# Third normalised block's square root earlier with read-outs on VectorE, the check's sums in the second pair, and second products of five groups by Strassen's seven products

## The chip, the cores and the metric

The kernel runs on 1 core of one Trainium2 chip. The metric is the device time of one execution in microseconds (us). Before the change it is 712.18 us, the median of three runs (710.34 to 712.77).

## What is computed

`x` has 2048 rows (S) of 512 columns (D); the hidden width F of the gated part is 1792. Cut to what matters:

```python
mod = (silu(c) @ w_mod).reshape(1, 6, 1, -1)
sa, ca, ga, sb, cb, gb = (mod[:, i] for i in range(6))
h = layernorm(x) * (1 + ca) + sa
a, b = h @ dft_hid_re.T, h @ dft_hid_im.T
x = x + ga * (dft_seq_re @ a - dft_seq_im @ b)
h = layernorm(x) * (1 + cb) + sb
x = x + gb * ((silu(h @ w1) * (h @ w3)) @ w2)
```

All of it is float32. The kernel multiplies in a rounded 32-bit format and writes each factor as a high part and a low rest, so that a product is three matmuls: high by high, high by low, low by high.

## The kernel before

The first 262 us of the profile are the Fourier part: it uses the symmetry of the transform matrices, and a check (`square`, `judge`) sums squares on the side, from which a flag `bad` is made; at the very end the program branches on it to a general version that needs no symmetry. The rest, about 436 us, is the gated part. That is where the change lies.

There the 2048 rows stand as four blocks t = 0 to 3 of 512 columns each (rows of `x` are the matmuls' moving columns). Two blocks make a pair: pair 0 is blocks 0 and 2, pair 1 is blocks 1 and 3. F is cut into seven groups g of 256, and a group has two factors (w1 and w3, 128 columns each twice) and one second product (w2).

- Groups 0 and 1 of pair 0 are done plainly (`up_block`), block 0 first, then block 2: `up(0, 0)`, `up(1, 0)`, eight second products of block 0, `up(0, 2)`, `up(1, 2)`. Here "the third block" is block 2; its normalisation (`ln2(2)`) must be done when `up(0, 2)` starts.
- Everything else is twelve items: groups 2 to 6 of pair 0, then groups 0 to 6 of pair 1. In an item each factor is done by Strassen's scheme in Winograd's form (`factor`), seven products in place of eight, called a1 to a7 for w1 and b1 to b7 for w3. One such unit is six matmuls. The second products are plain before the change (`down_unit`): for each of two blocks t and four slices d one unit of six matmuls in a bank of its own, and one read-out that scales by `gb` (`copy_by`, on ScalarE, line 335) into a tile `y`. Two read-outs fill a `y`, which GpSimd's queue adds to a sum in DRAM by an accumulating DMA (line 1146). Groups 5 and 6 of pair 1 add into the loaded sums `xr` instead and store the output.

The order on TensorE is written out by hand: the string `body` for an item lists its units, with a `y` where a second product of the item before is put between. `-b7`, `-b4`, `-b3` are units of the item before. ScalarE and VectorE get their own work in the order in which the planner's loop emits it. Two lists feed it beside the units: `jobs` (splitting weights into high and low) and `background` (the normalisations `ln2`, line 880 and around it). A step has a cost in us, and `advance` emits steps until the credit of a unit is used up; `pause` ends a turn. `behind(n, fn)` emits fn n units later. Each engine then executes its instructions strictly in that order.

The steps of `ln2` that matter: `a6` is a square root on ScalarE (32 by 16 numbers, with a table load ahead of it), `a6b` the reciprocal and its spread over the partitions on VectorE, `a7(i)` two multiplications on VectorE, `a8(i)` scale and shift on ScalarE, and then `chunk_parts` makes the high parts `h2h` (ScalarE) and the rests `h2l` (VectorE), which are what `up_block` multiplies.

Tiles of 512 KB come from a list of 50 slots (`take`, `give`), first in, first out; a slot that a `y` held is handed out again four units after its unit, and its next writer waits for the DMA that read it.

Of the kernel before, what the change touches and what calls it, by code (L numbers as in the profile page):

```python
# [8 lines left out]
F32 = mybir.dt.float32  # L9
# [33 lines left out]
def folded(nc, pools, c, cp, wmr, wmc, x, xt, ctr, cti, wdr, wdi, w1, w3, w2, out):  # L43
# [773 lines left out]
    def ln2(t):  # L817
# [97 lines left out]
        apart = t != PAIRS[0][0]  # L915
        pause = (0, None, 0.0, 0.0)
        for slots, fn, dve, act in (
# [17 lines left out]
            pause,  # L935
# [13 lines left out]
    def chunk_parts(queue, t, i, more=0):  # L949
# [8 lines left out]

        step(queue, 1 + more, highs, 0.0, 1.0)
# [153 lines left out]
    down_banks = [4, 4]  # L1113

    def down_unit(g, pair, t, d, key):
# [7 lines left out]
        for n in range(parts):  # L1123
            at = slice(n * N // parts, (n + 1) * N // parts)
            to = bank(down_banks[0] + turn[1] % down_banks[1])[:, at]
# [16 lines left out]
            else:  # L1142
                copy_by(ys[0][:, d % 2, :], to, gb[:, d : d + 1])
# [66 lines left out]

    def right(pair, n):
# [7 lines left out]
    def result(i, w, q, k, src):  # L1219
# [6 lines left out]
        times(v, v, src)  # L1226

# [9 lines left out]
        behind(2, lows)  # L1237

    def factor(i, w, n):
# [37 lines left out]
        if n == 3:  # L1277
            for x in wuse.pop(key).values():
                give(x)
            behind(1, lambda: give(st["x"]))  # L1280
            if w == "w3":
                for x in vs.pop(i):
                    behind(3, lambda x=x: give(x))
# [239 lines left out]
    for n, (j, k) in enumerate(steps):  # L1523
# [4 lines left out]
        for m in range(2):  # L1528
# [9 lines left out]
            if (j, k, m) == (0, NK - 1, 1):  # L1538
                for t in PAIRS[0]:
                    ln2(t)  # L1540
                    for i in range(2):
                        chunk_parts(background, t, i, 1)
# [36 lines left out]
    def down(g, pair, t, d, key):  # L1579
        drain(lambda: (key, "l") in done, jobs)  # L1580
        delayed()
        down_unit(g, pair, t, d, key)
# [14 lines left out]
    judge()  # L1597
# [8 lines left out]
    down_banks[:] = [6, 2]  # L1606
# [13 lines left out]

    def unit(kind, i, n):
# [12 lines left out]
        if (kind, n) == ("a", 1) and more:  # L1634
            load_w(("w1", *items[i + 1]))
        if (kind, n) == ("a", 6):
            load_w(("w2", g, pair))
        if (kind, n) == ("a", 3) and more:
            load_w(("w3", *items[i + 1]))
            weight_jobs(i + 1, "w1")  # L1640
        if (kind, n) == ("b", 2):
            plain_jobs(("w2", g, pair))
        if (kind, n) == ("b", 3):
# [7 lines left out]
            if more:  # L1651
                weight_jobs(i + 1, "w3")
            for t in PAIRS[pair]:
                seconds.extend((g, pair, t, d, ("w2", g, pair)) for d in range(ND))
# [5 lines left out]
    for i in range(len(items)):  # L1660
        body = "a6 a5 y a7 y y a4 y a3 y b1 y b2 y b6 b5 y"
        if i == turning:
            body = "y y y y y a6 y a5 y a7 y b1 b2 a4 b6 a3 b5"
        if i == len(items) - 1:
            body = "a6 a5 y a7 y y a4 y a3 b1 y b2 b6 b5 y b7 y b4 y b3 y y y y y y y y"
        head = "-b7 a1 -b4 -b3 a2 " if i == turning else "-b7 a1 a2 -b4 -b3 " if i else "a1 a2 "
# [813 lines left out]
```

## Time and profile before

| | |
|---|---|
| median of three runs | 712.18 us (710.34 to 712.77) |
| the profiled execution | 708.46 us |
| its span, first to last instruction | 706.7 us |
| mean granted TensorE clock | 0.991 |
| HBM read, written | 76.81 MB, 33.55 MB |
| accumulating DMAs `sum<-y` | 48 of 512 KB, median 5.6 us to landing |

The profile is of one execution. Busy times are a share of the span; PE is TensorE's matmuls, PEld its weight loads, DVE VectorE, ACT ScalarE, POOL GpSimd. A matmul's own duration overlaps that of the next one, so the pitch from start to start is what counts. In brackets behind a row of a timeline stands the idle time of its engine just before it and what ended it. DMA share is the mean busy share of the 16 DMA engines.

### The profile page before, as it was taken

The numbers are of one execution on the slowest core, as the hardware profiler recorded it, in microseconds if no ns is written. First come the engines' busy times: TensorE is split into PE (matmuls) and PEld (weight loads), VectorE is DVE, ScalarE is ACT, GpSimd is POOL, SyncE is SP. The second block draws the span as 40 slices with busy tenths as digits, with TensorE's granted clock in tenths as the row PEclk, the third lists the DMA queues.
The fourth block names the chain that finished last, engine by engine and source line by source line (L and its number), as shares of the span: only waits on it lengthen the run. The fifth ranks groups of instructions, "written<-read, shape, count | busy, mean of one in ns | idle before, by whom it ended". The sixth has DMA issues, their size and how long they took to land.

```text
span 706.7 us, 8912 instructions
## 1 busy us (share of the span) xinstructions
PE 686.3 (97%) x3152; PEld 564.7 (80%) x3152; DVE 548.3 (78%) x877; ACT 430.8 (61%) x709; POOL 119.4 (17%) x141
## 2 busy tenths in 40 slices
PE   7999999999999999899999999999999999999995
PEld 4898888888888888687888788787788888888784
DVE  5999679997999978579987886896865556664763
ACT  4998865545454655745677676867665565656420
POOL 1320253542524000200100101011010100101000
PEclk9999999999999999999999999999999999999998
DMA  8730299796678521522868558376763847537403
GB/s 266 211 120 1 77 373 328 251 307 229 207 283 287 168 86 41 92 58 64 209 114 199 89 130 153 61 156 137 239 136 73 180 62 175 111 69 162 137 0 124
DMA packets 38100, 108.93 MB, mean 154 GB/s; under 512 B 4896, under 2 KB 5152, under 8 KB 38048
## 3 DMA queue, kind: packets, MB, share of 16 engines
q0 software_dynamic: 12352, 43.00, 29.3%
q1 hardware_dynamic: 25264, 63.98, 27.5%
q10 hardware_dynamic: 432, 1.31, 0.5%
q8 instruction: 26, 0.43, 0.3%
q14 instruction: 26, 0.21, 0.1%
HBM read 76.81 MB, written 33.55 MB: 156 GB/s over the span
## 4 chain that ended last, share of the span: by engine, by line
PE 81%; DVE 7%; ACT 6%; issue 2%; DMA 2%; SPq 1%; ACTq 0%; DVEq 0%
PE bank L100 52%; PE bank L750 25%; PE bank L559 2%; PE bank L598 1%; DMA wmr<-in_wmr 1%; ACT xc L894 1%; PE bank L576 1%; DVE xc L96 1%; SPq L231 1%; ACT hf L87 1%; ACT y L335 1%; DVE v L96 0%; DVE hl L90 0%; ACT hm L501 0%; DMA w<-in_wdi 0%
## 5 line engine op out<-in xcount | busy, mean ns | idle before, releaser
L100 PE MATMUL bank<-hf,w2h 128*128 128x512 f32 (+1 forms) x452 | 140.9, 391 | 0.3
L1146 POOL DMA_DIRECT2D sum<-y x48 | 41.0, 855 | 390.1 <-ACT y L335 373.0
L100 PEld LDWEIGHTS bank<-hf,w2h 128*128 128x128 f32 x452 | 84.3, 188 | 22.1 <-DVE hf L90 3.4
L100 PE MATMUL bank<-hf,w2l 128*128 128x512 f32 (+1 forms) x226 | 87.6, 388 | 0.0
L87 ACT ACTIVATE hf<-v 128x512 fp32r<-128x512 f32 x56 | 35.3, 630 | 67.3 <-DVE v L96 62.7
L335 ACT ACTIVATE y<-bank,gb 128x512 f32<-128x512 f32 x96 | 64.9, 682 | 18.6 <-PE bank L100 18.3
L93 DVE TENSOR_TENSOR v<-bank,x 128x512 f32<-128x512 f32 x36 | 24.7, 685 | 34.9 <-PE bank L100 34.8
L750 PE MATMUL bank<-bh,us 128*128 128x512 f32 x128 | 49.9, 390 | 0.0
L93 DVE TENSOR_TENSOR x<-bank,x 128x512 f32<-128x512 f32 x36 | 24.7, 687 | 32.4 <-PE bank L100 28.7
L750 PE MATMUL bank<-bh,ul 128*128 128x512 f32 x128 | 49.8, 389 | 0.0
L750 PE MATMUL bank<-d,us 128*128 128x512 f32 x128 | 49.8, 389 | 0.0
L750 PE MATMUL bank<-d,uh 128*128 128x512 f32 x128 | 49.8, 389 | 0.0
L750 PE MATMUL bank<-l,us 128*128 128x512 f32 x128 | 49.8, 389 | 0.0
L750 PE MATMUL bank<-l,uh 128*128 128x512 f32 x128 | 49.8, 389 | 0.0
L100 PEld LDWEIGHTS bank<-hf,w2l 128*128 128x128 f32 x226 | 42.4, 188 | 8.4
L90 DVE TENSOR_TENSOR hf<-v,hf 128x512 fp32r<-128x512 f32 x56 | 38.5, 687 | 12.2 <-ACT hf L87 12.1
L170 POOL DMA_INDIRECT re<-in_ctr,mirror x32 | 35.8, 1117 | 66.2 <-DVE ul L90 39.5
L1224 ACT ACTIVATE v<-v 128x512 f32<-128x512 f32 x36 | 22.8, 632 | 38.8 <-DVE v L93 38.8
L87 ACT ACTIVATE x<-bank 128x512 f32<-128x512 f32 x72 | 41.4, 586 | 7.2 <-PE bank L100 6.5
L170 POOL DMA_INDIRECT im<-in_cti,mirror x32 | 32.7, 1023 | 35.3 <-PE bank L750 10.0
L100 PE MATMUL bank<-h2h,w1h 128*128 128x512 f32 x80 | 31.8, 397 | 1.5 <-ACT h2h L87 1.5
L100 PE MATMUL bank<-h2l,w1h 128*128 128x512 f32 x80 | 31.9, 399 | 0.8 <-DVE h2l L90 0.8
(246 smaller groups left out, 1775.2 us busy)
## 6 DMA issues: line engine op xcount, KB each, us to landing
sum<-y POOLq DMA_DIRECT2D x48, 512.0 KB, 5.6
w<-in_w SPq DMA_DIRECT2D x42, 512.0 KB, 4.5
re<-in_ctr SPq DMA_DIRECT2D x32, 256.0 KB, 5.0
im<-in_cti SPq DMA_DIRECT2D x32, 256.0 KB, 5.0
wmc<-in_wmc SPq DMA_DIRECT2D x8, 512.0 KB, 6.3
xr<-in_xt SPq DMA_DIRECT2D x8, 512.0 KB, 7.6
sum<-xr SPq DMA_DIRECT2D x8, 512.0 KB, 6.2
x<-in_x SPq DMA_DIRECT2D x11, 256.0 KB, 4.8
```

Source lines behind the costliest of these rows:

```text
L87: nc.scalar.activation(dst, src, AF.Copy, scale=scale)
L90: nc.vector.tensor_tensor(out=dst, in0=a, in1=b, op=OP.subtract)
L93: nc.vector.tensor_tensor(out=dst, in0=a, in1=b, op=OP.add)
L96: nc.vector.tensor_tensor(out=dst, in0=a, in1=b, op=OP.mult)
L100: nc.tensor.matmul(acc, lhs[a], rhs[b], start=first and n == 0, stop=last and n == len(PASSES) - 1, skip_group_check=more,)
L170: nc.gpsimd.indirect_dma_start(dst, None, rows, bass.IndirectOffsetOnAxis(ap=at, axis=0))
L231: queue.dma_start(raw_w[dt][q * 64 : (q + 1) * 64, m, :], w[i][par::2, q])
L335: nc.scalar.activation(dst, src, AF.Identity, scale=by)
L559: nc.tensor.matmul(halves(hb[k])[:, m, :], sides((hh, hl)[a][k])[:, dt, m, :], wu[dt][:, b, m, :], start=False, stop=dt % 2 == 1 and n == ...
L750: nc.tensor.matmul(acc[what, e], lhs, rhs, start=begin and i == 0, stop=(end or (turn and what == "x")) and i == len(terms) - 1, skip_grou ...
L1146: nc.gpsimd.dma_start(sums[t, d // 2], y, accum_op=OP.add)
L1224: behind(k != 0 or q == 0, lambda: nc.scalar.activation(v, src, AF.Silu))
```

## The change

Four parts:

1. **Third block.** For block 2 (`rushed`) the pauses around `a6` to `a8` and their costs go, and the two chunks' `h2h` and `h2l` are emitted with them. Read-outs `y` number 1 to 4 of each block's second products in pair 0's first groups go from ScalarE to VectorE (the new line 1153).
2. **The check.** `judge()` is called in the second item of pair 1, behind b4, in place of just ahead of `up(0, 2)`.
3. **Second products.** For groups 0 to 4 of pair 1 (`SEVEN`), w2's four quarters and the four quarters of `silu(gate) * up` are combined by Strassen's scheme as the factors are: seven units of two times three matmuls in banks 6 and 7 in place of eight units of six. Sums of a bank go on over several units, so each unit is read out from both banks (14 read-outs in place of 8), and each gives a `y` and a DMA (7 in place of 4). w2 gets `totals` and split sums, as w1 and w3 have.
4. **Order.** New strings for pair 1: in most of it two factor units between two second products, w1's loads and jobs placed anew, w3's jobs three units sooner, the last item's second products over five banks.

```diff
+        rushed = t == PAIRS[0][1]
...
-            pause,
+            *[pause] * (not rushed),
             (0, a6, 0.0, 2.8),
             pause,
             (0, a6b, 1.6, 0.0),
-            (0, lambda: a7(0), 1.2, 0.0),
-            *[pause] * apart,
-            (0, lambda: a8(0), 0.0, 1.4),
-            (0, lambda: a7(1), 1.2, 0.0),
-            *[pause] * apart,
-            (0, lambda: a8(1), 0.0, 1.4),
+            *[pause] * rushed,
+            (0, lambda: a7(0), 1.2 * (not rushed), 0.0),
+            *[pause] * (apart and not rushed),
+            (0, lambda: a8(0), 0.0, 1.4 * (not rushed)),
+            (0, lambda: a7(1), 1.2 * (not rushed), 0.0),
+            *([(0, fn, 0.0, 0.0) for fn in (None, chunk(t, 0)[0], None)] if rushed else [pause] * apart),
+            (0, lambda: a8(1), 0.0, 1.4 * (not rushed)),
...
+        if rushed:
+            for fn in (chunk(t, 0)[1], None, chunk(t, 1)[0], None, chunk(t, 1)[1], None):
+                step(background, 0, fn)
...
-                copy_by(ys[0][:, d % 2, :], to, gb[:, d : d + 1])
+                if pair == 0 and 1 <= g * ND + d <= 4:
+                    nc.vector.tensor_scalar(
+                        ys[0][:, d % 2, :], to, gb[:, d : d + 1], None, op0=OP.mult
+                    )
+                else:
+                    copy_by(ys[0][:, d % 2, :], to, gb[:, d : d + 1])
...
+    SEVEN = [(g, 1) for g in range(NG - 2)]
+    ORDER7 = (2, 5, 3, 1, 6, 7, 4)
+    LEFT7 = {1: "h0", 2: "h2", 4: "h3", 5: "s0", 6: "s1", 7: "s2", 3: "s3"}
+    TO7 = {2: (0, 0), 5: (1, 1), 3: (0, 1), 1: (0, 0), 6: (0, 1), 7: (1, 1), 4: (1, 0)}
...
+    def seven_parts(i, q, k):
...
+        t1, t2, t3, t4 = v[0, 0], v[1, 1], v[0, 1], v[1, 0]
+        behind(1, lambda: minus(t1, v[0, 1], v[0, 0]))
+        behind(2, lambda: high(5, t1))
+        behind(2, lambda: minus(t3, v[1, 1], v[0, 1]))
+        behind(3, lambda: low(5, t1))
+        behind(3, lambda: minus(t2, v[1, 1], t1))
+        behind(4, lambda: high(7, t3))
+        behind(4, lambda: minus(t4, v[1, 0], t2))
...
+    def seven_jobs(key):
...
+    def seven_unit(g, pair, n, key):
+        new = n in (1, 2, 5)
+        if new:
+            banks7[:] = [bank(6), bank(7)]
+        y = take(F32, "y")
...
+        for e, to in enumerate(banks7):
+            at = int(LEFT7[n][1]) * HALF + e * P
+            product(
+                to,
+                [flat(wuse[key][x])[:, at : at + P] for x in names],
+                [u[:, b, :] for b in range(2)],
+                new,
+                True,
+                not new,
+            )
+            d = 2 * which + e
+            copy_by(y[:, e, :], to, gb[:, d : d + 1])
+        give(u)
+        nc.gpsimd.dma_start(sums[t, which], y, accum_op=OP.add)
+        behind(4, lambda: give(y))
...
-    judge()
     up(0, 2)
...
+        if (kind, i, n) == ("b", turning + 1, 4):
+            judge()
...
+        if not more and kind == "a" and state[i, "w1"]["n"] == 7:
+            down_banks[:] = [6, 7, 0, 1, 2]
...
+        if i and items[i - 1] in SEVEN:
+            body = "a6 a5 a7 y a3 a4 y b1 b2 y b6 b5 y"
+        spread = i > 1 and items[i - 2] in SEVEN
+        if spread and i < len(items) - 1:
+            body = body.replace("a6", "a6 y", 1)
+        if i == len(items) - 2:
+            body = "a6 y a5 y a7 a3 y a4 b1 y b2 b6 y b5"
...
-            body = "a6 a5 y a7 y y a4 y a3 b1 y b2 b6 b5 y b7 y b4 y b3 y y y y y y y y"
+            body = "a6 a5 a7 a3 a4 b1 b2 y b6 y b5 y b7 y b4 y y b3 y y y y y y y y y y"
...
+        if spread and i < len(items) - 1:
+            head = "-b7 a1 y a2 -b4 y -b3 "
```

What this does to the order, at three places. The first is ScalarE ahead of `up(0, 2)`: `s` holds block 2's variances, `y` the second products of block 0 that are read out, `xc` block 2's two halves, and the last row is the table load ahead of the SiLU of `up(0, 2)`. Before:

```order
L87 ACTIVATE hf_379_2737<-v_377_2714 128x512
L880 ACT_TABLE_LOAD
L880 ACTIVATE s_2_377_2721<-s_2_377_2721,eps_128 32x16
L335 ACTIVATE y_381_2743<-bank4_382_2744,gb_152 128x512
L335 ACTIVATE y_381_2743<-bank5_383_2759,gb_152 128x512
L335 ACTIVATE y_384_2769<-bank6_385_2770,gb_152 128x512
L894 ACTIVATE xc_348_2564<-xc_348_2564,sb_150,cb1_151 128x512 x2
L335 ACTIVATE y_384_2769<-bank7_386_2780,gb_152 128x512
L335 ACTIVATE y_387_2790<-bank4_388_2791,gb_152 128x512
L894 ACTIVATE xc_360_2611<-xc_360_2611,sb_150,cb1_151 128x512 x2
L335 ACTIVATE y_387_2790<-bank5_389_2801,gb_152 128x512
L335 ACTIVATE y_390_2810<-bank6_391_2811,gb_152 128x512
```

and now:

```order
L880 ACT_TABLE_LOAD
L880 ACTIVATE s_2_377_2721<-s_2_377_2721,eps_128 32x16
L87 ACTIVATE hf_379_2738<-v_377_2714 128x512
L335 ACTIVATE y_381_2750<-bank4_382_2751,gb_152 128x512
L894 ACTIVATE xc_348_2564<-xc_348_2564,sb_150,cb1_151 128x512 x2
L87 ACTIVATE h2h_384_2772<-xc_348_2564 128x1024
L894 ACTIVATE xc_360_2611<-xc_360_2611,sb_150,cb1_151 128x512 x2
L87 ACTIVATE h2h_389_2796<-xc_360_2611 128x1024
L335 ACTIVATE y_390_2798<-bank5_393_2809,gb_152 128x512
L335 ACTIVATE y_394_2819<-bank6_395_2820,gb_152 128x512
L335 ACTIVATE y_394_2819<-bank7_396_2829,gb_152 128x512
L1103 ACT_TABLE_LOAD
```

The table load and the root stand ahead of `hf`. Before, seven read-outs stand ahead of the first `h2h` (it is the next row); now one does.

The second is VectorE at the same place. Before, from block 0's last product of the two factors on:

```order
L96 TENSOR_TENSOR v_377_2714<-v_377_2714,bank3_378_2723 128x512
L90 TENSOR_TENSOR hf_379_2737<-v_377_2714,hf_379_2737 128x512
L883 RECIPROCAL s_2_377_2721<-s_2_377_2721 32x16
L847 COPY w_2_382_2753<-s_2_377_2721 32x16 x4
L848 STREAM_TRANSPOSE stat_347_2556<-w_2_382_2753 128x512
L96 TENSOR_TENSOR xc_348_2564<-xc_348_2564,stat_347_2556 128x1024
L96 TENSOR_TENSOR xc_360_2611<-xc_360_2611,stat_347_2556 128x1024
L90 TENSOR_TENSOR h2l_393_2821<-xc_348_2564,h2h_392_2819 128x1024
L90 TENSOR_TENSOR h2l_396_2834<-xc_360_2611,h2h_395_2832 128x1024
L1006 TENSOR_REDUCE sq_2836<-chk_82 128x8
```

and now:

```order
L96 TENSOR_TENSOR v_377_2714<-v_377_2714,bank3_378_2724 128x512
L883 RECIPROCAL s_2_377_2721<-s_2_377_2721 32x16
L847 COPY w_2_379_2741<-s_2_377_2721 32x16 x4
L848 STREAM_TRANSPOSE stat_347_2556<-w_2_379_2741 128x512
L90 TENSOR_TENSOR hf_379_2738<-v_377_2714,hf_379_2738 128x512
L96 TENSOR_TENSOR xc_348_2564<-xc_348_2564,stat_347_2556 128x1024
L96 TENSOR_TENSOR xc_360_2611<-xc_360_2611,stat_347_2556 128x1024
L1153 TENSOR_SCALAR y_381_2750<-bank5_383_2763,gb_152 128x512
L1153 TENSOR_SCALAR y_385_2774<-bank6_386_2775,gb_152 128x512
L90 TENSOR_TENSOR h2l_387_2785<-xc_348_2564,h2h_384_2772 128x1024
L1153 TENSOR_SCALAR y_385_2774<-bank7_388_2787,gb_152 128x512
L1153 TENSOR_SCALAR y_390_2798<-bank4_391_2799,gb_152 128x512
```

The reciprocal passes `hf`, four read-outs come in, and the check's sums (L1006 and on) are gone from behind `h2l`.

The third is ScalarE in the second pair, from the first splitting of a group's w2 on. Before:

```order
L87 ACTIVATE w2h_829_5232<-w2_805_5104 128x1024
L87 ACTIVATE hf_831_5236<-v_797_5055 128x512
L335 ACTIVATE y_832_5238<-bank6_833_5239,gb_152 128x512
L87 ACTIVATE x_825_5210<-bank3_824_5203 128x512
L87 ACTIVATE x_835_5262<-bank5_834_5255 128x512
L335 ACTIVATE y_832_5238<-bank7_836_5264,gb_152 128x512
L87 ACTIVATE hf_837_5281<-v_798_5056 128x512
L87 ACTIVATE x_839_5290<-bank0_838_5283 128x512
```

and now:

```order
L87 ACTIVATE w2h_796_5014<-w2_773_4898 128x1024
L87 ACTIVATE hf_798_5021<-v_765_4815 128x512
L335 ACTIVATE y_799_5023<-bank6_789_4982,gb_152 128x512
L335 ACTIVATE y_799_5023<-bank7_790_4983,gb_152 128x512
L87 ACTIVATE w2sh_801_5035<-w2s_797_5016 128x1024
L87 ACTIVATE x_794_5003<-bank3_793_4996 128x512
L87 ACTIVATE w3h_803_5047<-w3_784_4959 128x1024
L87 ACTIVATE x_805_5056<-bank5_804_5049 128x512
L335 ACTIVATE y_809_5065<-bank6_807_5063,gb_152 128x512
L335 ACTIVATE y_809_5065<-bank7_808_5064,gb_152 128x512
L87 ACTIVATE w3sh_811_5077<-w3s_806_5058 128x1024
L87 ACTIVATE hf_812_5087<-v_766_4816 128x512
```

Read-outs come in pairs and there are more of them, `w2sh` is new, and `w3h` and `w3sh` stand ahead of the first pieces of `hf` of that group.

More of the change, by code (lines that the diff above doesn't have):

```diff
@@ L1650, in unit @@
                 other_operands()
-            if more:
+            if more and not early_w3(i):
                 weight_jobs(i + 1, "w3")
-            for t in PAIRS[pair]:
-                seconds.extend((g, pair, t, d, ("w2", g, pair)) for d in range(ND))
+            if (g, pair) in SEVEN:
+                seconds.extend((g, pair, n, ("w2", g, pair)) for n in ORDER7)
+            else:
+                for t in PAIRS[pair]:
+                    seconds.extend((g, pair, t, d, ("w2", g, pair)) for d in range(ND))
+        if (kind, n) == ("b", 6) and more and early_w3(i):
+            weight_jobs(i + 1, "w3")
         beside(1.36, FACTOR[kind][n])
```

100 lines of the change are left out of this document (87 added, 13 removed).

## The prediction

> **What bounds the kernel now.** I read the page first, then the windows, then TensorE's waits and its timeline. The page's busy times and the chain's shares:
>
> ```profile
> span 706.7 us, 8912 instructions
> PE 686.3 (97%) x3152; PEld 564.7 (80%) x3152; DVE 548.3 (78%) x877; ACT 430.8 (61%) x709; POOL 119.4 (17%) x141
> PE 81%; DVE 7%; ACT 6%; issue 2%; DMA 2%; SPq 1%; ACTq 0%; DVEq 0%
> PE bank L100 52%; PE bank L750 25%; PE bank L559 2%; PE bank L598 1%; DMA wmr<-in_wmr 1%; ACT xc L894 1%; PE bank L576 1%; DVE xc L96 1%; SPq L231 1%; ACT hf L87 1%; ACT y L335 1%; DVE v L96 0%; DVE hl L90 0%; ACT hm L501 0%; DMA w<-in_wdi 0%
> ```
>
> TensorE sets the time: 81% of the chain is matmuls, 52% of the span those of line 100, the gated part. A matmul taken out of there is worth its pitch, as long as nothing new holds the engine up. The pitch is read from the timeline of the first block, where `up(0, 0)` runs without a gap:
>
> ```profile
> 262.38 0.39 PE L100 MATMUL bank<-h2h,w1h 128*128 128x512 f32 x1
> 270.54 0.39 PE L100 MATMUL bank<-h2h,w3h 128*128 128x512 f32 x1
> ...
> 698.47 0.28 PE L100 MATMUL bank<-hf,w2l 128*128 128x256 f32 x1
> ```
>
> From the first matmul of w1's first quarter to the first of w3's second quarter are three blocks of twelve, 36 matmuls in 8.16 us: 0.2267 us each; a unit of six is 1.36 us. The gated part needs 192 matmuls of the plain `up`, 12 items of 84, and 14 times 48 second products, 1872 in all: 424.4 us. It lasts from 262.38 to the end of the last row, 698.75 us: 436.4 us, so 12 us in it are lost. The largest piece stands ahead of `up(0, 2)` (PE's timeline):
>
> ```profile
> 294.80 0.39 PE L100 MATMUL bank<-hf,w2l 128*128 128x512 f32 x1
> 296.71 0.51 PE L100 MATMUL bank<-h2h,w1h 128*128 128x512 f32 x1 [1.53 <-ACT h2h L87]
> 297.97 0.79 PE L100 MATMUL bank<-h2l,w1h 128*128 128x512 f32 x1 [0.76 <-DVE h2l L90]
> 298.56 0.63 PE L100 MATMUL bank<-h2h,w1l 128*128 128x512 f32 x1
> 300.70 0.50 PE L100 MATMUL bank<-h2l,w1h 128*128 128x512 f32 x1
> 295.00:300.00 5.00, 2.72 (x7) 0.75 1.02 193
> 300.00:305.00 5.00, 5.00 (x22) 0.91 0.71 107
> ```
>
> (The last two rows are of the windows of PE alone: busy, count, granted clock.) TensorE waits for block 2's `h2h`, then for `h2l`; then the granted clock is down and five matmuls from 298.56 to 300.70 go at 0.43 us each.
>
> **Third block: -4.2 us.** From 294.80 to 300.70 nine matmuls started where 26 would have fitted; eight steps at 0.2267 us are 1.8 us of the 5.9 us, so 4.1 us are lost, and 0.1 us more in the step behind. To see whether the new order ends it I walk the queues with these rows (ACT, then DVE):
>
> ```profile
> 281.62 0.60 ACT L1094 ACTIVATE v<-bank 128x512 f32<-128x512 f32 x1 [0.24 <-PE bank L100]
> 285.13 0.63 ACT L87 ACTIVATE hf<-v 128x512 fp32r<-128x512 f32 x1 [2.91 <-DVE v L96]
> 285.78 1.28 ACT L880 ACT_TABLE_LOAD   x1
> 287.29 1.82 ACT L335 ACTIVATE y<-bank,gb 128x512 f32<-128x512 f32 x3
> 290.49 1.53 ACT L894 ACTIVATE xc<-xc,sb,cb 128x512 f32<-128x512 f32 x2 [1.37 <-issue]
> 295.61 1.05 ACT L87 ACTIVATE h2h<-xc 128x1024 fp32r<-128x1024 f32 x1
> 284.02 0.25 DVE L840 TENSOR_REDUCE s<-q 32x16 f32<-32x64 f32 x1
> 284.41 0.69 DVE L96 TENSOR_TENSOR v<-v,bank 128x512 f32<-128x512 f32 x1
> 288.43 0.71 DVE L848 STREAM_TRANSPOSE stat<-w 128x512 f32<-128x512 f32 x1
> 289.18 2.36 DVE L96 TENSOR_TENSOR xc<-xc,stat 128x1024 f32<-128x1024 f32 x2
> 296.69 1.23 DVE L90 TENSOR_TENSOR h2l<-xc,h2h 128x1024 fp32r<-128x1024 f32 x1 [5.15 <-ACT h2h L87]
> ```
>
> Now the table load may start at 282.2, where ACT only waits for `v`, and is over when the variances `s` come at 284.3; the root ends at 284.7. DVE does the reciprocal behind `v` at 285.1, the spread until 286.8, `hf` until 287.5, both `xc` until 289.8 (291.5 before). ACT has `hf` and one read-out behind it by 286.5, shifts the first `xc` from 288.7, has the first `h2h` at 291.1 and the second at 293.6. DVE: read-outs of 0.7 us at 289.8 and 290.5, the first `h2l` at 292.4, two read-outs, the second `h2l` at 295.0. `up(0, 2)` can start at 295.0 and needs the second half 1.4 us later: no wait, and no lowered clock. Four read-outs come on DVE; no row of before has that form, and I price it between ACT's `y` (0.61 us each of 1.82 us for three) and DVE's `v<-v,bank` (0.69 us), at 0.7. They lie in the 5.15 us in which DVE waits for `h2h`. The read-outs left to ACT end at 296.1, the table load at 297.4, and the SiLU behind it is due at 297.9. A table load that turned out 1.5 us longer would still only touch that SiLU.
>
> [...]
>
> **The check: 0.** Its first and last VectorE instruction are, in DVE's timeline,
>
> ```profile
> 299.70 0.42 DVE L1006 TENSOR_REDUCE sq<-chk 128x8 f32<-128x256 f32 x1 [0.27 <-POOL sq L1005]
> 302.66 0.14 DVE L1026 TENSOR_SCALAR bad<-fine 1x1 int32<-1x1 f32 x1
> ```
>
> 3.1 us for small instructions that follow each other's results; TensorE has no wait there but the one it already had. In the second pair they stand behind b4's product; the next thing TensorE needs from DVE there is b3's sum, two units (2.7 us) on, which feeds products that come seven units later. Without that cover it is 3.1 us once.
>
> **Second products: -6.8 us.** Seven units in place of eight, in five groups: 5 x 6 = 30 matmuls at 0.2267 us. What they add per group goes to engines that are not full. Five stretches of 30 us, each about one group, and their groups:
>
> ```profile
> 540.00:570.00 30.00, 30.00 (x133) 24.57 (x132) 17.68 (x28) 18.17 (x27) 3.40 (x4) 1.00 0.60 123
> sum 150.00, PE 150.00 PEld 122.81 DVE 88.45 ACT 90.61 POOL 17.03; mean PE 30.00 PEld 24.56 DVE 17.69 ACT 18.12 POOL 3.41
> L335 ACT ACTIVATE y<-bank,gb 128x512 f32<-128x512 f32 x40 | 27.4, 684 | 10.4 <-PE bank L100 10.3
> L87 ACT ACTIVATE hf<-v 128x512 fp32r<-128x512 f32 x20 | 12.7, 633 | 23.2 <-DVE v L96 21.9 <-issue 1.3
> L87 ACT ACTIVATE w1sh<-w1s 128x1024 fp32r<-128x1024 f32 x5 | 5.3, 1063 | 0.6
> L90 DVE TENSOR_TENSOR hf<-v,hf 128x512 fp32r<-128x512 f32 x20 | 13.7, 686 | 3.5 <-ACT hf L87 3.5
> L87 ACT ACTIVATE x<-bank 128x512 f32<-128x512 f32 x30 | 17.6, 586 | 3.9 <-PE bank L100 3.9
> L90 DVE TENSOR_TENSOR w3s<-w3s,w 128x256 f32<-128x256 f32 x5 | 2.1, 426 | 0.2
> ```
>
> ACT: 6 read-outs of 0.684, 3 `hf` of 0.633, one `w2sh` of 1.06: +7.1 us, from 18.1 to 25.2 of a group of 21 units, 28.56 us: 88%. DVE: 3 rests and 4 differences of 0.69, 4 totals of 0.42, one `w2sl`, of the shape of `h2l`, 1.23: +7.7 us, from 17.7 to 25.4, 89%. Both fit, and both less tightly than these sums say, since instructions that follow each other start every 0.61 us (three `y` in 1.82), not 0.684.
>
> Fitting on average is not enough, because all seven units write the same two banks. After a bank's last matmul of a unit come two factor units and the other bank's three matmuls before it is written again: 2.7 + 0.7, less 0.2 for the last matmul's tail, 3.2 us. In these ACT must do two read-outs (1.25 us), so it may be late by 2.0 us. Ahead of a pair in the new order stand at most one weight copy, one `hf` and one `x` copy, 1.06 + 0.63 + 0.59 = 2.3 us, and the first of them starts while the unit still runs. Walking one group through both queues with these durations, I find the read-outs done 0.5 to 1.2 us before they are due, and b7's wait for its bank's copy (behind `w2sh`) has 0.5 us to spare. The closest case is another: the `y` of a1's neighbour takes the slot of the `y` two before it, 8.2 us earlier, and must wait for that DMA. The DMA view of 540 to 660 us, 16 sums and 12 other transfers of 512 KB:
>
> ```profile
> q0 software_dynamic: 2304, 8.39, 43.5%
> q1 hardware_dynamic: 1728, 6.29, 14.9%
> sum<-y POOLq DMA_DIRECT2D x16, 512.0 KB, 5.5
> ```
>
> A sum takes 0.435 x 120 / 16 = 3.26 us of all engines, a load 0.149 x 120 / 12 = 1.49 us. Seven sums and three loads are 27.3 us of 28.56: they fit, with 5% to spare. With 5.5 us to landing, and 1.5 more for a load between, it is 7.0 of 8.2 us. I take nothing for it, and keep both ends: 0 and, at 1.4 us a group, 7 us.
>
> **Small waits: -0.5 us.** The other 8 us are lost in pieces of half a us and less, such as this (PE's timeline):
>
> ```profile
> 323.50 0.39 PE L100 MATMUL bank<-h2h,w1l 128*128 128x512 f32 x1
> 324.11 0.50 PE L100 MATMUL bank<-th,w1sh 128*128 128x512 f32 x1 [0.23 <-ACT x L87]
> ```
>
> TensorE waits for an `x` copy that stands behind a `th` copy on ACT; with block 2 done earlier the `th` copies come sooner, 0.61 - 0.23 = 0.4 us. In the second pair the first product comes later behind b3 than before, which takes a little off each group; against it stand a7 one unit behind a6's copy in the first group, and slips in fuller queues. At best a third of the 8 us goes, at worst as much comes back: between -2.5 and +2.5 us; I take -0.5.
>
> **The sum.** 4.2 + 6.8 + 0.5 = 11.5 us off the profiled execution's 708.46 (span 706.7 and 1.8 around it): 697.0 us. That execution was 3.7 us under the median of the runs shown, 712.18, so the same step from the median gives 700.7 us, which I forecast.
>
> **Rivals.** (1) *Read-outs hold TensorE.* If ACT, at 88%, is late by 0.2 us at each of seven units, a group loses 1.4 us and the five lose 7 us: the second products give nothing, 707.7 us. For it: three of ACT's rows in a group wait for DVE and block those behind them (21.9 us idle ahead of 20 `hf`). Against it: the 2.0 us by which it may be late. (2) *The DMA engines become the bound* (slower). The sums alone need under (28.56 - 4.5) / 7 = 3.44 us each, and they took 3.26. If sums and loads slow each other by a third, to 4.4 us and 2.0, a group takes 7 x 4.4 + 6 = 36.8 us, 8.2 over 28.56; some four and a half groups lose 37 us, less the slack of the slots: some 25 us, 725 us. It beats the other terms from 3.8 us a sum on (7 x 3.8 + 4.5 = 31.1, 2.5 over, 11.5 in all). Against it: the 43.5% already hold overlapping loads. (3) *The third block keeps its wait*: a DMA or a bank that the walk doesn't see holds `h2h`; 704.9 us. For it: one read-out too late on DVE would push `h2l`. (4) Both (1) and (3): 711.9 us, no change.
>
> **How the numbers follow.** Forecast 0.70; (1) 0.12; (3) 0.06; (4) 0.04; (2) 0.08. A measurement of this kernel can tell about 0.3%, 2.1 us, from no change. The forecast, (1) and (3) are faster: 0.88; (4) is the same: 0.04; (2) slower: 0.08. The range takes the forecast's own ends, -2 us for small waits and 1 us for the median's own spread, 696.5, and upward (1) and (3), with 1 us for that spread: 708.5.
>
> **What would show it.** Right: no wait at the first `h2h` matmul and a clock of 1.00 around 295 us; 30 matmuls fewer on line 100; groups of about 28.6 us in the second pair; ACT and DVE near 85% there and a DMA share near 0.95. Wrong: TensorE waiting for `y` (ACT, 0.2 us and more) at banks 6 and 7, groups of 30 us, sums landing after 8 us and more, or a lowered clock in the second pair, which at 0.5 for 3.4 us would cost 1.7 us more each time.

## The result, and the profile after

The changed kernel takes 700.1 us (median of six runs, 698.81 to 703.31) where the kernel before, run beside it, took 711.9 us: a ratio of 0.9855, interval 0.9835 to 0.9874. It is about 1.4% faster, and the median is 0.6 us under the forecast. The profiled execution took 698.81 us, 9.65 less than that of before. The first two lines of its page:

```profile
span 697.0 us, 9026 instructions
PE 677.9 (97%) x3122; PEld 557.1 (80%) x3122; DVE 587.9 (84%) x945; ACT 451.4 (65%) x751; POOL 133.6 (19%) x156
```

30 recorded matmuls fewer, and 39.6 us more work on VectorE and 20.6 on ScalarE. To find where the 9.65 us went I lay the two TensorE timelines over each other, unit by unit, with the start of the gated part as zero. The first fence is the kernel before, at the first matmul of `up(0, 2)`'s w3, at a wait on the way and at a later unit of the first pair; the second is the changed kernel, at the gated part's start, at `up(0, 2)`, at the same w3 and, with three waits on the way, at the same later unit:

```profile
301.96 0.40 PE L100 MATMUL bank<-h2h,w3h 128*128 128x512 f32 x1
...
389.32 0.50 PE L100 MATMUL bank<-th,w1sh 128*128 128x512 f32 x1 [0.49 <-ACT x L87]
...
393.52 0.39 PE L100 MATMUL bank<-th,w1h 128*128 128x512 f32 x1
```

```profile
263.07 0.39 PE L100 MATMUL bank<-h2h,w1h 128*128 128x512 f32 x1
...
295.49 0.39 PE L100 MATMUL bank<-hf,w2l 128*128 128x512 f32 x1
295.71 0.39 PE L100 MATMUL bank<-h2h,w1h 128*128 128x512 f32 x1
...
298.43 0.39 PE L100 MATMUL bank<-h2h,w3h 128*128 128x512 f32 x1
...
359.22 0.50 PE L100 MATMUL bank<-th,w1h 128*128 128x512 f32 x1 [0.26 <-DVE v L93]
...
386.67 0.50 PE L100 MATMUL bank<-th,w1sh 128*128 128x512 f32 x1 [0.49 <-ACT x L87]
...
391.34 0.50 PE L100 MATMUL bank<-th,w1h 128*128 128x512 f32 x1 [0.29 <-DVE v L93]
```

Before, that w3 came 39.58 us after the part's start (301.96 - 262.38); now it comes 35.36 us after it. From 295.49 to 295.71 is one pitch: no wait for `h2h` or `h2l`. The rest of the first pair gives 1.35 us back: from that w3 to the later unit it took 91.56 us before and takes 92.91 us now; from there to the pair's end the two run alike. The wait for `x` at 386.67 us is not new: before, it stood at 389.32 us, of the same 0.49 us. The two waits for `v` have no like there. The second pair takes 6.23 us less. The table has all of it:

| piece | change, us |
|---|---|
| Fourier part (start of the gated part 262.38, now 263.07; same code) | +0.69 |
| third block | -4.22 |
| rest of the first pair | +1.35 |
| second pair, to the last matmul | -6.23 |
| behind the last matmul (8.2, now 7.0) | -1.24 |
| sum | -9.65 |

Two of five stretches of 30 us of the second pair, in the columns of the earlier windows (busy time and count of PE, PEld, DVE, ACT, POOL; clock; DMA share; GB/s), and the same matmul in two neighbouring groups:

```profile
495.00:525.00 30.00, 29.28 (x129) 23.62 (x128) 29.03 (x49) 22.03 (x35) 2.56 (x3) 1.00 0.58 150
555.00:585.00 30.00, 30.00 (x134) 24.82 (x133) 26.38 (x45) 25.05 (x41) 5.96 (x7) 1.00 0.94 186
```

```profile
581.55 0.39 PE L100 MATMUL bank<-hf,w2h 128*128 128x512 f32 x1
610.11 0.39 PE L100 MATMUL bank<-hf,w2h 128*128 128x512 f32 x1
```

In the steady groups TensorE never stops, and a group takes 28.56 us. The loss sits in the first two groups, where VectorE is the fullest (29.03 of the 30 us from 495 on): TensorE waits there twice for a `y`, and ScalarE's timeline shows what stood ahead of that read-out:

```profile
518.99 0.72 PE L100 MATMUL bank<-hf,w2sh 128*128 128x512 f32 x2 [0.56 <-ACT y L335]
...
540.54 0.72 PE L100 MATMUL bank<-hf,w2h 128*128 128x512 f32 x2 [0.39 <-ACT y L335]
```

```profile
517.30 1.06 ACT L87 ACTIVATE w1sh<-w1s 128x1024 fp32r<-128x1024 f32 x1
518.25 1.27 ACT L335 ACTIVATE y<-bank,gb 128x512 f32<-128x512 f32 x2
...
539.28 0.63 ACT L87 ACTIVATE hf<-v 128x512 fp32r<-128x512 f32 x1 [2.57 <-DVE v L90]
539.82 1.25 ACT L335 ACTIVATE y<-bank,gb 128x512 f32<-128x512 f32 x2
```

At 518 us a weight copy stands ahead of it, at 539 us an `hf` that waited 2.57 us for VectorE, which had the check's small instructions in front.

### The profile page after: what moved, and what is told of

Same layout as the page of the kernel before. It is cut to its first block, busy times and chain, and to the rows that moved or that the text cites. A ratio compares the mean times of both kernels' runs of the same rounds, so it can differ in the third digit from the quotient of the medians.

```text
span 697.0 us, 9026 instructions
## 1 busy us (share of the span) xinstructions
PE 677.9 (97%) x3122; PEld 557.1 (80%) x3122; DVE 587.9 (84%) x945; ACT 451.4 (65%) x751; POOL 133.6 (19%) x156
## 4 chain that ended last, share of the span: by engine, by line
PE 73%; DVE 11%; ACT 8%; issue 3%; DMA 3%; SPq 1%; another core or an unknown queue 1%; POOL 0%; ACTq 0%; POOLq 0%
PE bank L100 45%; PE bank L750 25%; PE bank L559 1%; DMA wmr<-in_wmr 1%; ACT y L335 1%; DMA sum<-y 1%; ACT hf L87 1%; DVE v L96 1%; PE bank L598 1%; DVE xc L96 1%; SPq L231 1%; ACT xc L894 1%; DVE x L93 1%; DVE w3s L90 1%; DVE v L93 1%
## 5 line engine op out<-in xcount | busy, mean ns | idle before, releaser
L100 PE MATMUL bank<-hf,w2h 128*128 128x512 f32 (+1 forms) x352 | 108.8, 390 | 0.5 <-ACT y L335 0.4
L87 ACT ACTIVATE hf<-v 128x512 fp32r<-128x512 f32 x71 | 44.3, 630 | 64.6 <-DVE v L96 53.8
L335 ACT ACTIVATE y<-bank,gb 128x512 f32<-128x512 f32 x118 | 76.5, 682 | 5.2 <-PE bank L100 5.1
L100 PEld LDWEIGHTS bank<-hf,w2h 128*128 128x128 f32 x352 | 65.4, 188 | 16.9 <-ACT y L335 2.2
L1160 POOL DMA_DIRECT2D sum<-y x28 | 24.0, 857 | 245.1 <-ACT y L335 125.1
L100 PE MATMUL bank<-hf,w2l 128*128 128x512 f32 (+1 forms) x176 | 68.1, 387 | 0.0
L90 DVE TENSOR_TENSOR hf<-v,hf 128x512 fp32r<-128x512 f32 x71 | 48.8, 687 | 13.8 <-ACT hf L87 13.8
L1352 POOL DMA_DIRECT2D sum<-y x35 | 29.8, 852 | 129.3 <-ACT y L335 124.9
L170 POOL DMA_INDIRECT re<-in_ctr,mirror x32 | 37.2, 1162 | 65.6 <-DVE ul L90 38.5
L87 ACT ACTIVATE x<-bank 128x512 f32<-128x512 f32 x72 | 41.5, 591 | 11.9 <-PE bank L100 11.8
L100 PEld LDWEIGHTS bank<-hf,w2l 128*128 128x128 f32 x176 | 33.0, 188 | 6.7
```

Source lines behind the costliest of these rows:

```text
L87: nc.scalar.activation(dst, src, AF.Copy, scale=scale)
L90: nc.vector.tensor_tensor(out=dst, in0=a, in1=b, op=OP.subtract)
L100: nc.tensor.matmul(acc, lhs[a], rhs[b], start=first and n == 0, stop=last and n == len(PASSES) - 1, skip_group_check=more,)
L170: nc.gpsimd.indirect_dma_start(dst, None, rows, bass.IndirectOffsetOnAxis(ap=at, axis=0))
L335: nc.scalar.activation(dst, src, AF.Identity, scale=by)
L1160: nc.gpsimd.dma_start(sums[t, d // 2], y, accum_op=OP.add)
```

## The experiments

All ratios are to the kernel before, run on the same chip beside the experiments of the same group: E1 to E4, E5 to E8, E9 to E11, and E12, each on one chip. "Gated part" is the time from the first matmul of `up(0, 0)` to the start of the last matmul, from each run's TensorE timeline: it leaves out the Fourier part and the tail, which without any edit there took 269.0 us together in E1's profiled execution and 274.3 in E8's, 5.2 us apart. It was 436.09 us before, 426.98 us in the changed kernel's first profile.

**E1, the changed kernel once more**, beside E2 to E4.

> The changed kernel once more, beside the kernel before on the same chip, so that the next three have something to be compared with. My theory: 11.8 us faster than before (700.1 us against 711.9 measured), and in its trace no wait ahead of the third block and groups of 28.6 us in the second pair. If the first measurement flattered it, as the profiled execution (698.8 against 708.5, 9.7 us) could mean, 8 to 9 us faster.

698.24 us (697.85 to 699.23), ratio 0.9858 [0.9832, 0.9884], gated part 427.46 us. The ratio repeats. The kernel before took 707.17 us beside it, so the medians differ by 8.9 us and not by 11.8: the smaller of the two sizes named, and close to the 9.65 us of the profiled executions.

**E2, without the third block's part.**

```diff
-        rushed = t == PAIRS[0][1]
+        rushed = False
...
-                if pair == 0 and 1 <= g * ND + d <= 4:
+                if False:
```

(and the background makes both chunks again)

> Part 1 undone alone: the pauses and the late root are back, and all read-outs of pair 0 are on ScalarE; the check stays in the second pair, Strassen's second products stay. My theory (the third block is worth 4.2 us by itself): 704.3 us, TensorE idle for 1.5 us ahead of the first h2h matmul, and a clock of 0.5 for 3.4 us behind it. A little less (703.5 us) if the check's absence from VectorE there helps h2l. Rival: the third block's time comes back elsewhere, since all later work waits for VectorE anyway: 700 to 701 us.

702.5 us (701.3 to 705.23), ratio 0.9919 [0.9895, 0.9944]. The waits are back at their old size, in TensorE's timeline and one row of its windows (busy, count, granted clock):

```profile
295.48 0.39 PE L100 MATMUL bank<-hf,w2l 128*128 128x512 f32 x1
297.39 0.51 PE L100 MATMUL bank<-h2h,w1h 128*128 128x512 f32 x1 [1.53 <-ACT h2h L87]
298.65 0.50 PE L100 MATMUL bank<-h2l,w1h 128*128 128x512 f32 x1 [0.75 <-DVE h2l L90]
...
301.46 0.39 PE L100 MATMUL bank<-h2h,w3h 128*128 128x512 f32 x1
...
295.00:300.00 5.00, 2.72 (x11) 1.00 1.06 179
```

The medians differ by 4.3 us, as expected, but partly by luck: the gated part is only 2.03 us longer (429.49 us); the rest is the Fourier part, 1.1 us later, and a tail 1.5 us longer. And the lowered clock that was expected, 0.50 for 3.41 us in the profile before (297.50 to 300.91 us), did not come. Behind waits as long as those of before the granted clock stays at 1.00, where before it was 0.75 in the same window. From the last matmul ahead of `up(0, 2)` to its first matmul of w3 E2 takes 5.98 us (295.48 to 301.46), the kernel before 7.16 (294.80 to 301.96), the changed kernel 2.94 (295.49 to 298.43). So the waits cost 3.04 us, and the other 1.18 of the 4.22 us are the lowered clock, which the profiled execution before had and E2's had not. Beside E2 the part gains 3.04 us at its place and hands about one of them back.

**E3, without the second products and their order; E9, the same with the check at its old place.**

```diff
-    SEVEN = [(g, 1) for g in range(NG - 2)]
+    SEVEN = []
```

(with the strings, loads and banks of before; E9 also calls `judge()` ahead of `up(0, 2)` again, so it is the kernel before with the third block's part alone)

> Parts 3 and 4 undone: plain second products everywhere in before's order of units, parts 1 and 2 kept. My theory (30 matmuls of 0.2267 us less what waits in the first group gave back): 4.5 to 6.8 us slower than the changed kernel, 704.6 to 706.9 us, with the second pair's groups back at 30.2 us. Rival (the read-outs cost what the matmuls saved): no slower than the changed kernel, 700 us. Rival (the order of part 4 gains beside the matmuls): 708 us and over.

711.1 us (709.26 to 713.96), ratio 1.0043 [1.0026, 1.0061]: slower than before, though the third block's wait is gone, and in the band of the last rival, that the new order gains beside the matmuls. Its gated part is 437.34 us, 3.0 us over E9's. The reason has one place, and it is the check. TensorE's and VectorE's timelines of E3:

```profile
543.30 0.50 PE L100 MATMUL bank<-hf,w2h 128*128 128x512 f32 x1 [2.19 <-DVE hf L90]
...
544.72 0.63 PE L100 MATMUL bank<-th,w1sh 128*128 128x512 f32 x1
545.14 0.63 PE L100 MATMUL bank<-tl,w1sh 128*128 128x512 f32 x1
```

```profile
536.77 0.41 DVE L1015 TENSOR_REDUCE sq<-chk 128x8 f32<-128x256 f32 x1
...
539.71 0.14 DVE L1035 TENSOR_SCALAR bad<-fine 1x1 int32<-1x1 f32 x1
...
542.55 0.69 DVE L90 TENSOR_TENSOR hf<-v,hf 128x512 fp32r<-128x512 f32 x1
```

The check's 3.1 us of small instructions stand ahead of a rest `hf` that a plain second product needs at once: 2.19 us of waiting, and then matmuls at a pitch of 0.42 us, with a granted clock of 0.72 from 545 to 550 us.

> The kernel before with the third block's part alone: read-outs on VectorE, second products and their order as before, and the check's sums at their old place. It is E3 without the move of the check. E3's trace shows TensorE waiting 2.19 us at 541 us for an hf behind the check's small VectorE instructions, and eight matmuls at a lowered clock after it, 4.0 us in all, which would be what swallowed the third block's 4.2 us. Theory: without the move this is gone; 4.2 us less, some 1 us of it given back in small waits of the first pair: ratio 0.9945 to 0.9965, no gap of over 0.3 us between 535 and 545 us. Rival: the order of before gives the third block's gain back by itself, wherever the check stands; then 1.000 to 1.005, as E3.

707.18 us (706.54 to 708.08), ratio 0.9988 [0.9975, 1.0], above the expected band, and by its interval hardly to be told from the kernel before: alone, the third block's part gains next to nothing in the whole time. The gap at 541 us is gone and the gated part is 434.37 us, 3.0 us under E3's and 1.72 us under that of before. So the theory holds for the check, and not for the amount given back: of the 4.2 us that the profile before lost there some 2.5 are lost again in small waits.

**E4, the check at its old place** (`judge()` ahead of `up(0, 2)`, all else as changed).

> Part 2 undone alone: the check's sums are ahead of the third block's second half again. My theory: the 3.1 us on VectorE fall behind h2l, where VectorE then has sums that nothing waits for yet, so the total stays (700.1 us), and the wait for the read-outs y of 0.4 us at 539.8 us, behind the check's sums in the second pair, is gone: 0 to 0.7 us faster. Rival: the check at its old place delays the splitting of the sums and with it the first items' waits: 1 to 2 us slower.

698.91 us (698.36 to 699.35), ratio 0.9865 [0.984, 0.9891], gated part 427.79 us: no difference that can be measured. It is a trade, though. The wait at 540 us is gone, and there is another, behind `up(1, 2)`:

```profile
320.18 0.50 PE L100 MATMUL bank<-th,w1sh 128*128 128x512 f32 x1 [0.41 <-ACT x L87]
```

E4 and E9 differ in the second products and their order (parts 3 and 4) alone: 434.37 - 427.79 = 6.6 us in the gated part. No run has one of these two parts without the other.

**E5, the four read-outs of each block back on ScalarE** (the condition replaced by `False`, as in E2).

> The four read-outs of each block that went to VectorE are on ScalarE again, the order is otherwise that of the change. My theory: ScalarE has three more read-outs (0.6 us each) ahead of the second h2h; the second h2l, due 1.4 us into up(0, 2), comes some 2 us later: TensorE waits 0.5 to 1.5 us there, 0 to 2.5 us slower than the changed kernel in all, the upper end if the clock falls. Rival: the root's place alone ends the wait, and the read-outs on VectorE are for nothing: same time, no wait at the third block.

701.91 us (700.91 to 703.47), ratio 0.9889 [0.987, 0.9907]. The gated part is 427.39 us, the same as E1's: one wait of 0.36 us for a `y` at 296 us, and small waits fewer elsewhere. The 3 us and more by which the median lies above E1's lie ahead of the gated part (264.08 us) and behind it (9.1 us), where this edit touches nothing; they say nothing of the read-outs. The changed kernel was not run beside E5 to E8, and E6 and E7, on the same chip as E5, have ratios of 0.988 as well. The rival holds: at the third block nothing waits for `h2h` or `h2l`.

**E6 and E7, more transfers**: two and four extra loads of 512 KB per group of seven products, on SP's queue, from w2 to a tile that nobody reads.

```diff
+        if ORDER7.index(n) in (0, 3):
+            spare = dram.tile([P, 2, N], F32, name=f"spare_{g}_{n}")
+            nc.sync.dma_start(spare, w2[g])
```

(E6; E7 has `in (0, 1, 3, 5)`)

> Two more transfers of 512 KB, DRAM to DRAM, in each of the five groups of Strassen's second products, which nothing waits for. The engine time of a group's transfers goes from 27.3 us to some 30.3 us or more, over the 28.56 us of TensorE. Theory 'TensorE bounds with 5 per cent to spare': the group is then bound by the DMA engines, 2 us a group and up to 9 us in all, about 706 to 709 us, with TensorE waiting for read-outs y whose slots are still held by an earlier sum. Theory 'the slots and queues absorb it': under 1 us slower.

> The same with four more transfers in each of the five groups: 33.3 us of engine time or more against 28.56 us. If the DMA engines bound: 4.7 us a group and more, 720 us and over. If they do not, the kernel stays within 2 us of the changed one, and the 27.3 us that I added up from the packets are not engine time that adds.

E6 took 701.74 us (700.17 to 703.47), ratio 0.9879 [0.986, 0.9897]; E7, with twice as much, 701.08 us (700.35 to 702.68), 0.9882 [0.9865, 0.9899]. Their gated parts, 427.67 and 427.46 us, are E1's. The DMA view from 555 to 645 us, of the changed kernel and of E7, and a window of E7:

```profile
DMA packets 4681, 17.12 MB, mean 190 GB/s; under 512 B 512, under 2 KB 512, under 8 KB 4676
q0 software_dynamic: 3236, 11.81, 78.6%
...
sum<-y POOLq DMA_DIRECT2D x22, 512.0 KB
```

```profile
DMA packets 5016, 23.44 MB, mean 260 GB/s; under 512 B 713, under 2 KB 713, under 8 KB 4810
q0 software_dynamic: 3193, 11.57, 67.9%
...
sum<-y POOLq DMA_DIRECT2D x23, 512.0 KB
```

```profile
585.00:615.00 30.00, 30.00 (x134) 24.79 (x133) 26.38 (x44) 24.83 (x41) 5.96 (x7) 1.00 1.01 252
```

A share of 1.01, and TensorE without a gap. The same sums that took 0.786 x 90 / 22 = 3.22 us of all engines take 2.66 us when more is to be moved. The time of packets was here no fixed cost that adds up, so "27.3 of 28.56 us" was no measure of what was left.

**E8, more work on ScalarE**: one 128x512 copy ahead of each pair of read-outs, into a tile that the read-out then writes over.

```diff
+        copy(y[:, 0, :], u[:, 0, :].bitcast(F32))
         for e, to in enumerate(banks7):
```

> One more ScalarE copy of 128 x 512 (0.6 us) ahead of each pair of read-outs in the five groups, its output overwritten by the read-out: 4.2 us a group, from 24.5 to 28.7 us of 28.56 us of TensorE. My theory: the read-outs have 0.5 to 1.2 us to spare in a group, so one such copy alone would pass, but seven use up what is idle, and the group becomes ScalarE's: 1 to 2 us a group, 705 to 710 us, with waits for y and x at every unit. Rival: ScalarE is already at its end, each copy shows in full: 4.2 us a group, 720 us. Rival: no effect.

710.65 us (709.18 to 714.24), ratio 1.0011 [1.0, 1.0023]; gated part 438.24 us, 10.8 us over E1's: all that the change brought. One of E8's windows, and the same matmul in two neighbouring groups:

```profile
585.00:615.00 30.00, 29.61 (x128) 23.33 (x127) 24.98 (x40) 27.36 (x45) 5.97 (x7) 1.00 0.88 175
```

```profile
591.58 0.50 PE L100 MATMUL bank<-hf,w2h 128*128 128x512 f32 x1
621.58 0.50 PE L100 MATMUL bank<-hf,w2h 128*128 128x512 f32 x1
```

Seven copies, some 4.1 us of ScalarE a group (at 0.59 us, the changed kernel's `x` copies), make the steady group 30.00 us instead of 28.56, 1.44 us as the theory had it, with ScalarE at 91% of the time and not at 100%: what counted here was how long one pair of read-outs was held up, not the share. TensorE waits six times for a `y` from 490 to 690 us, 5.6 us in all. The rest of the loss lies in the first two groups and in the last, and takes the total just over the 710 us expected.

**E10, the check in the last item; E11, with the first group's w1 jobs one unit later as well.**

```diff
-        if (kind, i, n) == ("b", turning + 1, 4):
+        if (kind, i, n) == ("a", len(items) - 1, 4):
```

> The changed kernel with the check's sums behind a4 of the last item, where VectorE is at 24.5 of 30 us, in place of the second item of the second pair. Theory: the 0.55 us gap at 540 us (y behind an hf that waits for VectorE) goes, and nothing takes its place: 0.5 to 0.8 us less than the changed kernel, ratio 0.9845 to 0.9855 where that has 0.9855 to 0.986. Rival: the 3.1 us of small instructions make the last group's waits, about 650 us, longer, and the time stays the same or grows by up to 1 us.

> E10, and in the first item after the first group of seven products the jobs for the next w1 begin one factor unit later, so that on ScalarE the read-outs of the second product stand ahead of the copy w1sh and not behind it. Theory: TensorE's wait for y at 518 us (0.5 us, 0.8 us with its step behind) goes, and the x wait at 524 us is at most as long: 0.5 to 0.8 us less than E10, ratio 0.9835 to 0.985. Rival: the weight jobs that start later hold the next copies of x, and the wait only moves to about 524 us: same as E10.

E10: 698.27 us (697.5 to 698.51), ratio 0.9858 [0.9835, 0.988], gated part 426.78 us. The 540 us wait is gone and nothing came for it, 0.68 us less in the gated part than E1, little more than the 0.48 us by which E1 and the first profile of the same kernel differ; the ratio can't tell. E11: 701.03 us (699.81 to 702.17), ratio 0.9898 [0.9876, 0.992], gated part 427.66 us. The 518 us wait is gone, and three others stand at 520, 523 and 532 us (0.25, 0.93 and 0.44 us): the rival, and 0.9 us worse. Its other 2 us are again the tail (9.0 us, E10's 6.8).

**E12, E10 with the first pair's w3 jobs one unit later** (begun behind a6, not behind b3).

> E10, and in the first pair the jobs for the next w3 begin one factor unit later (behind a6, not behind b3), so that on ScalarE the copy w3h stands behind the first of two x copies and not ahead of it. In the changed kernel TensorE waits 0.49 us for that x at 386 us and again at 448 us, where also xc of the next block is shifted, each with 0.25 us just ahead and 0.1 us behind; and 0.3 us for v, which stands behind w3sl on VectorE, at 358, 390 and 452 us. Theory: the small waits of the first pair come from the order on ScalarE alone; then both x waits go and the v waits stay: about 1.3 us less than E10, ratio 0.984 where E10 had 0.9858. Rival: w3l and w3sl on VectorE move back by the same 1.1 us, v behind them with them, and the three v waits grow from 0.3 to 0.8 us and more: same as E10 or slower.

699.18 us (697.76 to 699.46), beside runs of before at 710.29 us: ratio 0.9839 [0.9825, 0.9852], gated part 425.91 us, the shortest of all. One of the two `x` waits is gone, the one at 386 us; the `v` waits grew by 0.2 us in all; the `y` wait at 479 us is in E10 too (0.33 us). TensorE's waits (in all, times, longest) in the first pair, to 485 us, in the kernel before (from 301 us), in the changed kernel and in E12 (from 297 us), and ScalarE's timeline of E12 at the wait that stayed:

```profile
PE bank L100 <- ACT x L87: 1.2, 3, 0.5
PE bank L100 <- DVE v L93: 0.3, 1, 0.3
```

```profile
PE bank L100 <- ACT x L87: 1.0, 2, 0.5
PE bank L100 <- DVE v L93: 0.8, 3, 0.3
```

```profile
PE bank L100 <- DVE v L93: 1.0, 3, 0.4
PE bank L100 <- ACT x L87: 0.5, 1, 0.5
PE bank L100 <- ACT y L335: 0.4, 1, 0.4
```

```profile
447.23 1.04 ACT L87 ACTIVATE h2h<-xc 128x1024 fp32r<-128x1024 f32 x1
448.18 0.61 ACT L87 ACTIVATE hf<-v 128x512 fp32r<-128x512 f32 x1
448.70 0.57 ACT L87 ACTIVATE x<-bank 128x512 f32<-128x512 f32 x1
```

Both `x` waits of the changed kernel stand in the kernel before too, where a third, of 0.23 us, is the one at 324 us; of the three `v` waits it has one. The place that `w3h` left was taken by an `h2h` of the next blocks, 1.04 us as well. By its interval E12 can't be told from E1; by the gated part it is 1.55 us shorter than E1, most of it in the waits named, and 0.87 us shorter than E10, where 1.3 were expected.

## Why the prediction was right, and where it was not

**The third block, -4.2 us: right at its place between these two executions, -4.22 us, with luck in the clock.** The walk of both queues had the two `h2h` done at 291.1 and 293.6 us and the first `h2l` at 292.4; less the 0.69 us by which this run was late ahead of it, they were done at 291.1, 293.6 and 292.4. ScalarE's and VectorE's timelines of the changed kernel:

```profile
282.93 1.28 ACT L880 ACT_TABLE_LOAD   x1
285.00 0.31 ACT L880 ACTIVATE s<-s,eps 32x16 f32<-32x16 f32 x1 [0.79 <-DVE s L840]
290.77 1.06 ACT L87 ACTIVATE h2h<-xc 128x1024 fp32r<-128x1024 f32 x1
293.27 1.06 ACT L87 ACTIVATE h2h<-xc 128x1024 fp32r<-128x1024 f32 x1
```

```profile
290.18 1.41 DVE L1153 TENSOR_SCALAR y<-bank,gb 128x512 f32<-128x512 f32 x2
291.86 1.23 DVE L90 TENSOR_TENSOR h2l<-xc,h2h 128x1024 fp32r<-128x1024 f32 x1 [0.28 <-ACT h2h L87]
```

The table load is over before the variances come, and TensorE arrives at 295.7. Two read-outs on VectorE take 1.41 us, the 0.7 each that was put in by bounds. Rival 3 is excluded by the timeline, and E2 shows that the waits return when the part is undone. But the price held the lowered clock as a sure consequence of waits of 1.53 and 0.76 us, and E2, with the same waits, kept its clock: there the part is worth 3.04 us, nearer to the 2.7 us that the two waits alone come to in the rows of before (1.91 and 1.26 us from start to start, less one step of 0.2267 us each). The other 1.18 us came from the execution that was profiled before. E5 shows that the read-outs on VectorE, which the walk needed, were not needed: without them the gated part is as long.

**The check, 0: right as a sum, for another reason.** The cover named was the distance to b3's sum. But TensorE needs pieces of `hf` from VectorE sooner than that: the wait at 540 us is for a read-out behind an `hf` that VectorE held up. What happened is an exchange: 0.39 us of waiting at 540 us for 0.41 us at 320 us (E4). E3 shows the case without cover: in the order of before the same place costs 2.19 us of waiting and a lowered clock, 3.0 us in all beside E9, which has 0.28 us of waiting at 319 us instead. That this is near the 3.1 us that the prediction named for that case is chance, since those were the length of the check and no clock.

**Second products, -6.8 us: right.** -6.6 us between E9 and E4, with the new order in it, steady groups of 28.56 us, which is 126 matmuls at 0.2267 us, ScalarE at 25.05 of 30 us (84%) and VectorE at 26.38 (88%). The walk of one group, with read-outs done 0.5 to 1.2 us before they are due, fits the steady groups and not the first two, where TensorE waits 0.56 and 0.39 us for a `y`. Rival 1 named the mechanism that lies next, and E8 shows how near it is: some 0.6 us more in front of each read-out pair and the whole gain is gone.

**Small waits, -0.5 us: this step failed in sign.** They came to about +1.9 us: 1.35 in the first pair, 0.57 in the second (6.23 where 6.8 was due); inside the bounds of 2.5 either way. Even the one wait that it took away, for `x` at 324 us, is gone for half of the reason given: with block 2 as early and the check at its old place (E4 and E9) it is there, 0.41 and 0.28 us, and with the check moved and block 2 late (E2) too, 0.23 us. It takes both parts. New are the waits for `v`, 0.26 us at 359 and 0.29 at 391, each some 0.55 us with the slower matmuls behind it, and five places where units take 0.1 to 0.3 us longer. They come with the third block's part: E2, without it, has neither of the two waits, and E9, which has no other part, has both (0.25 and 0.29 us). The step had looked only at the waits of before and not walked the items behind `up(1, 2)`, whose background work also moved. That the new waits come from the normalisations falling into other units is argued and not shown. E12 shows the cause of the wait for `x` at 387 us, a weight copy ahead of an `x` copy on ScalarE, but that wait is an old one.

**The time itself** came out closer than its terms, by luck: the sum was 11.5 us, the two profiled executions differ by 9.65, the medians by 11.8 here and by 8.9 in E1. The forecast took the 11.5 off a median 3.7 us above the profiled execution; the changed kernel's profiled execution lies only 1.3 us under its median. In both measurements of the changed kernel the ratio is 0.986.

**Rival 2, the DMA engines** (725 us) is refuted by E7: four more loads of 1.49 us a group, 4.7 us beyond the 1.3 to spare, cost nothing. In these runs the busy share of the 16 DMA engines did not show the room that was left: 190 GB/s at a share of 0.94 (the changed kernel), 260 GB/s at 1.03 (E7), both from 555 to 645 us.

## What to carry to other kernels

When a stall is taken out of queues that run in order, as ScalarE's did here (the `y` at 539.82 us stood behind an `hf` that had waited 2.57 us for VectorE), walk on through the next items too: other waits opened there when the stall ended, and 1.35 of the 4.22 us were handed back in pieces of 0.1 to 0.6 us. Before moving small serial work such as the check, ask which consumer stands behind it in its queue in that very order: the same 3.1 us cost 0.4 us of waiting beside one order and 2.2 us and a lowered clock beside another. Compare experiments by the stage that they touch, since start and tail alone moved the whole by 2 to 5 us. And price a lowered clock as a chance and not as a sure cost: look for it in more than one profile.

## What the runs showed of the hardware

- **A DMA share near 1 was not full here.** At 0.94 there was room for 13 more loads of 512 KB in 90 us (E7, 555 to 645 us, share 1.03); the accumulating transfers' packets became shorter (3.22 to 2.66 us of all engines each), and TensorE's gated part stayed as long (427.46 us, as in E1).
- **Waits of the same length came with a lowered clock in one execution and not in another.** The kernel before waited 1.53 and 0.76 us ahead of `up(0, 2)`, and the granted clock fell to 0.75 and 0.91 in two windows of 5 us; E2 waited 1.53 and 0.75 us there and kept 1.00. E3's 2.19 us were followed by 0.72 (545 to 550 us), and its TensorE goes on at 0.42 us a matmul from 544.72 us; behind 0.56 us at 519 us the changed kernel's windows keep 1.00. Narrower windows of the profile before show one stretch of 3.41 us at 0.50, from 297.50 to 300.91 us, which is where the 0.5 for 3.4 us of the prediction and of E2's expectation can be read; ahead of it TensorE had been idle for 1.53 us and for the first 0.28 of the 0.76. What made the difference between that execution and E2's is not shown by these runs.
- **The tail came in two lengths.** From the last matmul's start to the end of the span it is 6.7 to 7.6 us in eight of the profiles (the changed kernel, E1, E4, E6, E7, E8, E10, E12) and 8.2 to 9.1 us in six (before, E2, E3, E5, E9, E11), with the same last steps in it. E2, E5 and E11 have the changed kernel's last item and yet the longer tail; what it waits for is not in the trace's rows and, with one profile for most kernels, whether it belongs to the build or to the execution stays open. It makes 2 us of E5's and E11's distance from E1.
